# Fused attention, mixture of experts and FFN: hops and stores in steps of their own, one program order to the end, and weight splits spread over two steps

## The chip, the cores and the metric

The kernel runs on one core of a Trainium2 chip. The metric is the device time of one execution in microseconds. Before the change three runs took 1039.25, 1039.57 and 1040.21 us; their median is 1039.57 us.

## The reference

Three stages follow each other, all in float32, over 4 x 576 = 2304 tokens of 512 numbers:

```python
# linear attention, 8 heads of 64, with an RMS norm
kv = np.einsum('bhsd,bhse->bhde', k, v)
out = np.einsum('bhsd,bhde->bhse', q, kv)
out = out / np.sqrt(np.mean(out * out, axis=-1, keepdims=True) + 1e-06) * g_norm

# mixture of experts: the best 2 of 8 experts by noisy logits
for e in range(8):
    for k in range(2):
        mask = top2[:, k] == e
        h = np.maximum(x[mask] @ w1[e], 0.0)              # 512 -> 1024
        y[mask] += top2_w[mask, k, None] * (h @ w2[e])    # 1024 -> 512

# gated FFN, 512 -> 1536 -> 512
g = x @ w_gate
return (g / (1 + np.exp(-g)) * (x @ w_val)) @ w_out
```

Each expert has room for 640 tokens (`CAP`); tokens beyond that are handled by a branch, `spill`, that these inputs skip. The FFN's weights arrive as 64-bit floats.

## The kernel before, in words

**Precision.** Each float32 operand is split into a rounded half `hi` (written by ACT) and a remainder `lo` (a subtraction on DVE). A product is three matmuls on PE: hi·hi, hi·lo and lo·hi. `piece_split` (L624) does this for one piece of weights: L630 on ACT, then L632 on DVE, 128 x 1024 each.

**Blocks and steps.** The experts' tokens are worked in 16 blocks of 256 or 384 columns (`blocks`, L676 ff.): 256, 256, 384, 384, then 384, 256 four times, then 384, 384, 256, 256. A block has 8 steps. Step k computes `u` (`expert_up`, 12 matmuls, L752), from it `hh` on ACT (L761) and `hl` on DVE (L762), and runs `down` (L771) for step k-1: per 128 tokens three matmuls of 512 columns into `y`, with hh, hh and hl as the loaded operand. That makes 128 expert steps. Then the FFN runs in 6 groups `m` of 384 tokens with 12 steps each: `ug` and `uv` (12 matmuls each, L825), `sg`, `a` and `gl` on DVE, `gh` on ACT, and `down` again.

**What else a step does** stands in a table, `at(step, fn)` (L966 ff.):
- `piece_load` 3 or 4 steps ahead on SP (raw_w), and `piece_split` at the step itself.
- `narrow` (L650 ff.): 36 chunks that turn the FFN's weights from 64 to 32 bits. A DMA brings `d_..` in; three steps hold seven DVE operations (L658 to L668); the third also holds an addition on POOL (L669) and the DMA that stores the result (L670, SP). Chunks are spread over the 384-column blocks 2 to 13.
- `x_gather` (POOL, L701), then `x_quarters`: SP writes the gathered rows out as `xq` (L721) and reads them back turned by quarters (L722). This pair of DMAs is the hop.
- `x_halves` (L724): DVE transposes 32 x 32 blocks (`turn`, L691), ACT rounds (`xh`, L684), DVE subtracts (`xl`, L686): the operands of the next block.
- for the FFN the same with `y_mix` (two gathers), `y_sum` (ACT L801, DVE L802, then the hop) and `y_halves` (L691, L812, L813).
- `expert_out` stores y from ACT (L784, L787).
- `spill` (L861) after FFN step 1: four small DVE operations, a load of their result `toti` into a register of every engine (L869) and a branch on it (L870).

**Order.** `InOrder` (L31) keeps PE, ACT, DVE and SP in the program's order while `on` is set. It is set until step 16 (`PINNED`; the loop over `pinned` at L1152 clears it). From there to the end of the FFN the scheduler orders each engine's instructions by its own simulation. POOL is left to the scheduler throughout, since its `on` is never set. Buffers come from rings: tag "S" (6 of 128 x 1024, raw weights and `d_..`), tag "R" (5 of 128 x 512: xg, turn, f_.., ys, ya, yb).

Of the kernel before, what the change touches and what calls it, by code (L numbers as in the profile page):

```python
# [9 lines left out]
F32 = mybir.dt.float32  # L10
# [39 lines left out]
def attn_moe_ffn(ctx: ExitStack, tc: tile.TileContext, q, k, v, g_norm, w_gate, w_noise, noise, w1, w2,  # L50
# [32 lines left out]
        return wpool.tile([P, 1024], F32, name=nm, tag="W")  # L83

    def st_tile(nm):
        return pool.tile([P, 1024], F32, name=nm, tag="S", bufs=6)

    def row_tile(nm):
        return pool.tile([P, 512], F32, name=nm, tag="R", bufs=5)

    def xt_tile(nm):
        return pool.tile([P, 4, 384], F32, name=nm, tag="X", bufs=4)
# [555 lines left out]
    def narrow(src, dst, i):  # L648
        nm = f"{dst.name}_{i}"
        n = 512  # L650
        raw = st_tile("d_" + nm).bitcast(I32).rearrange("p (n t) -> p n t", t=2)
        SP.dma_start(raw.rearrange("p n t -> p (n t)"),
                          src.rearrange("a b -> (a b)").rearrange("(i p n) -> i p n", p=P, n=n)[i].bitcast(I32))
        f = row_tile("f_" + nm)
        fi, hw, lw = f.bitcast(I32), raw[:, :, 1], raw[:, :, 0]

        def one():
            V.tensor_scalar(fi, hw, 0x7FFFFFFF, None, op0=OP.bitwise_and)  # L658
            V.tensor_scalar(hw, hw, -2 ** 31, None, op0=OP.bitwise_and)
# [12 lines left out]
        return one, two, three


    blocks = [(0, 0, 256), (1, 0, 256), (0, 256, CAP - 256), (1, 256, CAP - 256)]
# [37 lines left out]
        gather_rows(x, xd[0:TP * P] if bk < 2 else xd, slot_tok[:, 0 if bk < 2 else 1, k:k + 1])  # L713
        XT[bk, "x", i] = x

    def x_quarters(bk, i):
        to_quarters(XT[bk, "x", i], f"xq{bk}_{i}")

    def to_quarters(x, nm):
        put, get = by_quarter(nm)  # L720
        SP.dma_start(put, x.rearrange("p (g k) -> p g k", g=4))  # L721
        SP.dma_start(x, get)  # L722

    def x_halves(bk, *tiles):  # L724
        if bk not in XT:
# [73 lines left out]
    def y_sum(t):  # L799
        a, b = XT.pop(("y", t))  # L800
        ACT.activation(a, a, AF.Copy, scale=wts[:, t, 0:1])  # L801
        V.scalar_tensor_tensor(b, b, wts[:, t, 1:2], a, op0=OP.mult, op1=OP.add)  # L802
        to_quarters(b, f"yq{t}")
        XT["y", t] = b

    def y_halves(t):
# [161 lines left out]
    def at(step, fn, *args):  # L968
        todo.setdefault(step, []).append((fn, args))

    starts = [NF * i for i in range(NB)]
    first_ffn = NF * NB
    for e in range(1, E):
        for i, (key, src, c) in enumerate(expert_pieces(e)):
            s0 = 7 + i if e == 1 else NF * 2 * (e - 1) + (i if e == E - 1 else 2 * i)
            at(s0 - 4, piece_load, key, src, c)
            at(s0, piece_split, key)
    for i, (key, src, c) in enumerate(ffn_pieces()):
        s0 = first_ffn - 14 + i if i < 15 else first_ffn - 10 + i
        at(s0 - 3, piece_load, key, src, c)  # L980
        at(s0, piece_split, key)
    if wide:
        halves = []
        for srcdst in ((u_gate, ug32), (u_val, uv32), (u_out, uo32)):
            halves += [(*srcdst, i) for i in range(DM * FU // (P * 512))]
        def start_narrow(i):
            XT["n", i] = narrow(*halves[i])

        slots = []
        for bk in range(2, NB - 1):  # L990
            slots += [starts[bk] + 8 * i // NARROW[blocks[bk][2]] for i in range(NARROW[blocks[bk][2]])]
        for i in range(len(halves)):
            st = slots[i * len(slots) // len(halves)]
            at(st - 4, start_narrow, i)
            for c in range(3):
                at(st + c, lambda i=i, c=c: XT["n", i][c]())
    for bk in range(2, NB):
        p = starts[bk - 1]
        n = blocks[bk][2] // P
        for i in range(n):  # L1000
            if bk > 2:
                at(p + 1, x_gather, bk, i)
            if bk > 3:
                at(p + 2 + i, x_quarters, bk, i)
            at(p + (5 if bk == 2 else 4) + i, x_halves, bk, i)
    for m in range(NM):
        p = first_ffn + NU * (m - 1) if m else first_ffn - NF - 3
        for i in range(3):
            lag = 2 * i + 2 if m else i + 1
            at(p + lag, y_mix, 3 * m + i)  # L1010
            at(p + lag + 2, y_sum, 3 * m + i)
            at(p + lag + 4, y_halves, 3 * m + i)

    def run_todo(step):
# [131 lines left out]
    for bk in range(NB):  # L1146
        for f in range(NF):
            st = starts[bk] + f
            if st == PINNED:
                later()  # L1150
                drain(routes)
                for x in pinned:  # L1152
                    x.on = False
            if st < PINNED:
                later()
                expert_up(bk, f)
# [59 lines left out]
```

## Time and profile before

| what | before |
|---|---|
| median of 3 runs | 1039.57 us |
| the profiled execution | 1039.84 us, its span 1038.2 us |
| busy in the span | PE 990.1 (95%), DVE 570.2 (55%), ACT 350.8 (34%), POOL 174.6 (17%) |
| PE's granted clock | 0.93 on average up to 145.93 us, 1.00 from there |
| expert blocks 2 to 15 | 145.93 to 573.15 us |
| FFN | 573.15 us to the end |

The profile comes from one execution and its span leaves out 1.64 us around it. "Busy" counts instructions that execute; an operation that waits in an engine's queue shows as idle time of that engine, with the name of what ended the wait (`<-`). DVEq, PEq and SPq are the engines' sequencers. Line numbers are those of the kernel before.

### The profile page before, as it was taken

The numbers are of one execution on the slowest core, as the hardware profiler recorded it, in microseconds if no ns is written. First come the engines' busy times: TensorE is split into PE (matmuls) and PEld (weight loads), VectorE is DVE, ScalarE is ACT, GpSimd is POOL, SyncE is SP. The second block draws the span as 40 slices with busy tenths as digits, with TensorE's granted clock in tenths as the row PEclk, the third lists the DMA queues.
The fourth block names the chain that finished last, engine by engine and source line by source line (L and its number), as shares of the span: only waits on it lengthen the run. The fifth ranks groups of instructions, "written<-read, shape, count | busy, mean of one in ns | idle before, by whom it ended". The sixth has DMA issues, their size and how long they took to land. (4 is left out here: it accounts for less than half of the span.)

```text
span 1038.2 us, 14809 instructions
## 1 busy us (share of the span) xinstructions
PE 990.1 (95%) x5689; PEld 894.6 (86%) x5690; DVE 570.2 (55%) x1080; ACT 350.8 (34%) x620; POOL 174.6 (17%) x171
## 2 busy tenths in 40 slices
PE   7988799998999999999999999999999999999998
PEld 7877687987898887889798979999999999999997
DVE  1869888687674758578637452342342432432222
ACT  3654434333524334352237331231321321321211
POOL 2414243322221221212221110100100100100000
PEclk9989899999999999999999999999999999999999
DMA  9995665866766767577657330310310310400000
GB/s 258 296 257 139 213 214 202 281 205 222 243 227 220 227 208 232 197 219 238 213 189 259 122 103 1 112 41 1 112 42 1 119 35 1 126 7 1 31 1 31
DMA packets 114508, 151.60 MB, mean 146 GB/s; under 512 B 15936, under 2 KB 75328, under 8 KB 114432
## 3 DMA queue, kind: packets, MB, share of 16 engines
q1 hardware_dynamic: 99536, 113.51, 35.8%
q0 software_dynamic: 6736, 22.29, 6.7%
q10 hardware_dynamic: 8160, 14.81, 4.0%
q8 instruction: 45, 0.74, 0.3%
q14 instruction: 31, 0.25, 0.1%
HBM read 108.64 MB, written 41.94 MB: 145 GB/s over the span
## 5 line engine op out<-in xcount | busy, mean ns | idle before, releaser
L752 PE MATMUL u<-xh,hi_w 128*128 128x384 f32 (+1 forms) x448 | 140.3, 314 | 2.2 <-ACT xh L684 2.2
L752 PE MATMUL u<-xl,hi_w 128*128 128x384 f32 (+1 forms) x448 | 140.4, 313 | 1.6 <-DVE xl L686 1.6
L752 PE MATMUL u<-xh,lo_w 128*128 128x384 f32 (+1 forms) x448 | 140.0, 313 | 0.0
L831 DVE TENSOR_TENSOR sg<-ug,sg 128x384 f32<-128x384 f32 x72 | 40.0, 555 | 154.2 <-ACT sg L830 154.2
L771 PE MATMUL y<-hi_w,hh 128*128 128x512 f32 x290 | 115.5, 398 | 5.0 <-ACT hh L761 4.8
L771 PE MATMUL y<-lo_w,hh 128*128 128x512 f32 x290 | 114.6, 395 | 0.0
L771 PE MATMUL y<-hi_w,hl 128*128 128x512 f32 x290 | 98.3, 401 | 5.4 <-DVE hl L762 5.2
L825 PE MATMUL uv<-mh,hi_uv 128*128 128x384 f32 x288 | 96.7, 336 | 1.6 <-DVE sg L831 1.4
L825 PE MATMUL ug<-mh,hi_ug 128*128 128x384 f32 x288 | 96.8, 336 | 0.4 <-PEq L870 0.4
L825 PE MATMUL ug<-mh,lo_ug 128*128 128x384 f32 x288 | 96.9, 336 | 0.0
L825 PE MATMUL uv<-mh,lo_uv 128*128 128x384 f32 x288 | 96.7, 336 | 0.0
L825 PE MATMUL ug<-ml,hi_ug 128*128 128x384 f32 x288 | 96.6, 335 | 0.0
L825 PE MATMUL uv<-ml,hi_uv 128*128 128x384 f32 x288 | 96.4, 335 | 0.0
L752 PEld LDWEIGHTS u<-xl,hi_w 128*128 128x128 f32 x448 | 84.4, 188 | 8.4 <-DVE xl L686 3.3
L752 PEld LDWEIGHTS u<-xh,hi_w 128*128 128x128 f32 x448 | 84.3, 188 | 8.0 <-ACT xh L684 3.9
L752 PEld LDWEIGHTS u<-xh,lo_w 128*128 128x128 f32 x448 | 84.4, 188 | 3.9
L834 ACT ACTIVATE gh<-a 128x384 fp32r<-128x384 f32 x72 | 37.8, 525 | 145.3 <-DVE a L832 145.3
L761 ACT ACTIVATE hh<-u 128x384 fp32r<-128x384 f32 (+1 forms) x113 | 49.0, 436 | 111.5 <-PE u L752 106.1
L830 ACT ACTIVATE sg<-ug 128x384 f32<-128x384 f32 x72 | 35.1, 488 | 151.7 <-PE ug L825 151.6
L632 DVE TENSOR_TENSOR lo_w<-raw_w,hi_w 128x1024 fp32r<-128x1024 f32 x48 | 61.9, 1290 | 37.1 <-ACT hi_w L630 37.1
L762 DVE SCALAR_TENSOR_TENSOR hl<-u,hh 128x384 fp32r<-128x384 f32 (+1 forms) x113 | 55.3, 489 | 36.7 <-ACT hh L761 36.7
L630 ACT ACTIVATE hi_w<-raw_w 128x1024 fp32r<-128x1024 f32 x48 | 50.9, 1059 | 68.1 <-DMA raw_w<-in_moe_w_dram 50.6
(420 smaller groups left out, 1993.5 us busy)
## 6 DMA issues: line engine op xcount, KB each, us to landing
raw_w<-in_moe_w_dram SPq DMA_DIRECT2D x56, 512.0 KB, 4.2
yd<-ys ACTq DMA_DIRECT2D x40, 256.0 KB, 2.7
xq<-xg SPq DMA_DIRECT2D x30, 256.0 KB, 3.8
xg<-xq SPq DMA_DIRECT2D x30, 256.0 KB, 4.4
d_ug<-in_moe_w_gate_dram SPq DMA_DIRECT2D x12, 512.0 KB, 4.6
d_uv<-in_moe_w_val_dram SPq DMA_DIRECT2D x12, 512.0 KB, 4.3
d_uo<-in_moe_w_out_dram SPq DMA_DIRECT2D x12, 512.0 KB, 4.4
yq<-yb SPq DMA_DIRECT2D x18, 256.0 KB, 2.7
```

The lines of the kernel that those rows point to most:

```text
L630: ACT.activation(hi.bitcast(F32R), raw, AF.Copy)
L632: V.tensor_sub(lo.bitcast(F32R), raw, hi)
L752: PE.matmul(pu, w[a][:, c, (f % 2) * P:(f % 2 + 1) * P], xs[b][:, c, 0:n], start=(k == 0), stop=(k == 11))
L761: ACT.activation(hi.bitcast(F32R), pu, AF.Relu)
L762: V.scalar_tensor_tensor(lo.bitcast(F32R), pu, 0.0, hi, op0=OP.max, op1=OP.subtract)
L771: PE.matmul(ACC[key][i], hs[a][:, i * P:(i + 1) * P], w[b][:, fi], start=(f == 0 and k == 0), stop=(f == nf - 1 and k == 2), skip_group_ch ...
L825: PE.matmul(pu, w[a][:, c, (f % 2) * P:(f % 2 + 1) * P], xs[b][:, c], start=(k == 0), stop=(k == 11))
L830: ACT.activation(sg, ps[0], AF.Sigmoid)
L831: V.tensor_mul(sg, ps[0], sg)
L834: ACT.activation(hi.bitcast(F32R), a, AF.Copy)
```

## The change

1. `x.on = False` at step 16 goes: PE, ACT, DVE and SP keep the program's order to the end.
2. The hop is split: `x_put` at step p-2+i and `x_get` at p+1+i (p is the first step of the block before; both were at p+2+i), and `x_gather` of blocks 4 and up moves from p+1 to p-4. `x_halves` stays at p+4+i. `y_get` gets a step of its own after `y_sum`.
3. The store of `narrow` gets a fourth step, one after the POOL addition.
4. `split_at` leaves `hi` at its step and puts `lo` one step later, for all pieces but those of expert 1.
5. Ring S has 7 buffers, ring R has 9, and `dynamic_dma_scratch_size` is set to 4096, which leaves room for them.

```diff
-        return pool.tile([P, 1024], F32, name=nm, tag="S", bufs=6)
+        return pool.tile([P, 1024], F32, name=nm, tag="S", bufs=7)
...
-        return pool.tile([P, 512], F32, name=nm, tag="R", bufs=5)
+        return pool.tile([P, 512], F32, name=nm, tag="R", bufs=9)
...
             POOL.tensor_add(f, f, lw.bitcast(F32))
+
+        def four():
             SP.dma_start(dst.rearrange("a b -> (a b)").rearrange("(i p n) -> i p n", p=P, n=n)[i], f)
...
         SP.dma_start(put, x.rearrange("p (g k) -> p g k", g=4))
-        SP.dma_start(x, get)
+        return lambda: SP.dma_start(x, get)
...
+    def split_at(step, key, apart=True):
+        if apart:
+            late = []
+            at(step, piece_split, key, late)
+            at(step + 1, lambda: V.tensor_sub(*late.pop()))
+        else:
+            at(step, piece_split, key)
...
-            at(s0, piece_split, key)
+            split_at(s0, key, e > 1)
...
-                at(p + 1, x_gather, bk, i)
+                at(p + 1 if bk < 4 else p - 4, x_gather, bk, i)
             if bk > 3:
-                at(p + 2 + i, x_quarters, bk, i)
+                at(p - 2 + i, x_put, bk, i)
+                at(p + 1 + i, x_get, bk, i)
...
+            at(p + lag + 3, y_get, 3 * m + i)
...
-                for x in pinned:
-                    x.on = False
...
-    nc = bacc.Bacc("TRN2", target_bir_lowering=False, num_devices=1)
+    nc = bacc.Bacc("TRN2", target_bir_lowering=False, num_devices=1, dynamic_dma_scratch_size=4096)
```

DVE, second half of block 11, where block 12's operands are made (`xl12`, from three x tiles) beside the `hl11` of the steps. Before:

```order
L691 STREAM_TRANSPOSE turn_4658<-xg12_0_4558 128x512
L762 SCALAR_TENSOR_TENSOR hl11_4_4644<-u11_4_4630,hh11_4_4643 128x256
L686 SCALAR_TENSOR_TENSOR xl12_4657<-turn_4658,gcol_73,xh12_4656 128x4x128
L632 TENSOR_TENSOR lo_w2_7_1_4916<-raw_w2_7_1_4756,hi_w2_7_1_4915 128x1024
L691 STREAM_TRANSPOSE turn_4693<-xg12_1_4560 128x512
L762 SCALAR_TENSOR_TENSOR hl11_5_4685<-u11_5_4671,hh11_5_4684 128x256
L632 TENSOR_TENSOR lo_w1_7_2_4957<-raw_w1_7_2_4785,hi_w1_7_2_4956 128x1024
L691 STREAM_TRANSPOSE turn_4729<-xg12_2_4562 128x512
L658 TENSOR_SCALAR f_uo32_117_3_4655<-d_uo32_117_3_4653 128x512
L686 SCALAR_TENSOR_TENSOR xl12_4657<-turn_4693,gcol_73,xh12_4656 128x4x128
L762 SCALAR_TENSOR_TENSOR hl11_6_4717<-u11_6_4703,hh11_6_4716 128x256
```

After:

```order
L44 SCALAR_TENSOR_TENSOR hl11_4_4647<-u11_4_4633,hh11_4_4646 128x256
L44 STREAM_TRANSPOSE turn_4660<-xg12_0_4386 128x512
L44 SCALAR_TENSOR_TENSOR xl12_4659<-turn_4660,gcol_73,xh12_4658 128x4x128
L44 SCALAR_TENSOR_TENSOR hl11_5_4690<-u11_5_4676,hh11_5_4689 128x256
L44 TENSOR_TENSOR lo_w1_6_3_4651<-raw_w1_6_3_4529,hi_w1_6_3_4650 128x1024
L44 STREAM_TRANSPOSE turn_4699<-xg12_1_4388 128x512
L44 SCALAR_TENSOR_TENSOR xl12_4659<-turn_4699,gcol_73,xh12_4658 128x4x128
L44 SCALAR_TENSOR_TENSOR hl11_6_4723<-u11_6_4709,hh11_6_4722 128x256
L44 STREAM_TRANSPOSE turn_4734<-xg12_2_4390 128x512
L44 SCALAR_TENSOR_TENSOR xl12_4659<-turn_4734,gcol_73,xh12_4658 128x4x128
L44 SCALAR_TENSOR_TENSOR hl11_7_4760<-u11_7_4746,hh11_7_4759 128x256
```

Before, `hl` and a weight remainder stand between a `turn` and its `xl`, and pieces of `narrow` (`f_uo32`) between two tiles. Now each `xl` follows its `turn` at once, and the next `hl` stands behind it.

SP, where the x tiles of a block make their hop among stores of `narrow` (`ug32`) and loads. Before, block 4:

```order
L721 DMA xq4_0_2295<-xg4_0_2247 128x4x128
L721 DMA xq4_1_2326<-xg4_1_2249 128x4x128
L722 DMA xg4_0_2247<-xq4_0_2295 128x512
L721 DMA xq4_2_2377<-xg4_2_2251 128x4x128
L722 DMA xg4_1_2249<-xq4_1_2326 128x512
L670 DMA ug32_115<-f_ug32_115_6_2123 128x512
L652 DMA d_ug32_115_11_2456<-in_moe2_w_gate_dram 128x1024
L622 DMA raw_w1_3_1_2523<-in_moe_w1_dram 128x4x256
L722 DMA xg4_2_2251<-xq4_2_2377 128x512
```

After, block 5:

```order
L44 DMA xq5_0_2465<-xg5_0_2378 128x4x128
L44 DMA ug32_115<-f_ug32_115_7_2214 128x512
L44 DMA xq5_1_2498<-xg5_1_2380 128x4x128
L44 DMA raw_w1_3_1_2529<-in_moe_w1_dram 128x4x256
L44 DMA ug32_115<-f_ug32_115_8_2258 128x512
L44 DMA d_uv32_116_0_2576<-in_moe2_w_val_dram 128x1024
L44 DMA xg5_0_2378<-xq5_0_2465 128x512
L44 DMA raw_w2_3_1_2612<-in_moe_w2_dram 128x2x512
L44 DMA d_uv32_116_1_2622<-in_moe2_w_val_dram 128x1024
L44 DMA xg5_1_2380<-xq5_1_2498 128x512
```

Before, one, two and four rows lie between the put (`xq4_i<-xg4_i`) and the get (`xg4_i<-xq4_i`) of tiles 0, 1 and 2. Now five and six lie between those of tiles 0 and 1.

DVE, the four operations of `spill`. Before, they stand in block 1, behind the count of the routed tokens (`base_f`):

```order
L44 TENSOR_TENSOR base_f_113<-base_f_113,rk2_1509 128x8
L44 TENSOR_TENSOR oh@2_1502<-oh@2_1502,rk@2_1545 128x144
L863 TENSOR_SCALAR over_6021<-base_f_113 128x8
L868 CAST cnti_6026<-base_f_113 128x8
L865 TENSOR_REDUCE tot_6023<-over_6021 128x1
L867 CAST toti_6025<-tot_6023 128x1
L44 SCALAR_TENSOR_TENSOR hl1_0_1550<-u1_0_1475,hh1_0_1549 128x256
```

After, they stand behind FFN step 1 (`a_1`, `gl_1`) and a weight remainder:

```order
L44 TENSOR_TENSOR sg0_1_5999<-ug0_1_5973,sg0_1_5999 128x384
L44 TENSOR_TENSOR a0_1_6000<-uv0_1_5986,sg0_1_5999 128x384
L44 TENSOR_TENSOR gl0_1_6005<-a0_1_6000,gh0_1_6004 128x384
L44 TENSOR_TENSOR lo_uo_4_5959<-raw_uo_4_5860,hi_uo_4_5958 128x1024
L44 TENSOR_SCALAR over_6021<-base_f_113 128x8
L44 TENSOR_REDUCE tot_6023<-over_6021 128x1
L44 CAST toti_6025<-tot_6023 128x1
L44 CAST cnti_6026<-base_f_113 128x8
L878 TENSOR_LOAD toti_6025
L879 COMPARE_AND_BRANCH
```

The result that all engines load before the branch is now made where the program has it, some 540 rows later on DVE.

## Rows read from the trace of the kernel before

**Rows 1.** The page's head: span of the profiled execution.

```profile
span 1038.2 us, 14809 instructions
```

**Rows 2.** Stretches of expert blocks 2 to 15: us, busy us of each engine, PE clock, DMA.

```profile
145.93:213.18 67.25, 64.93 (x332) 58.16 (x331) 54.17 (x100) 26.94 (x42) 19.59 (x12) 1.00 0.70 231
213.18:279.95 66.77, 61.04 (x323) 51.91 (x322) 49.09 (x75) 25.58 (x38) 15.73 (x12) 1.00 0.73 233
279.95:337.95 58.00, 57.56 (x315) 50.80 (x315) 38.67 (x66) 22.11 (x33) 11.85 (x9) 1.00 0.67 218
337.95:399.64 61.69, 57.43 (x311) 50.15 (x310) 41.25 (x67) 24.12 (x35) 13.19 (x11) 1.00 0.67 218
399.64:573.15 173.51, 169.94 (x932) 151.16 (x933) 121.17 (x197) 71.78 (x106) 38.25 (x31) 1.00 0.68 219
```

**Rows 3.** The chain of waits in a steady FFN step: start, us, what.

```profile
704.74 2.09 PE ug L825 x12
...
708.91 0.70 PE y('m', 1)_0_6938 L771 x3
```

**Rows 4.** Timeline of a 256-column step: start, us, engine, line.

```profile
560.84 0.39 ACT L761 ACTIVATE hh<-u 128x256 fp32r<-128x256 f32 x1
...
561.12 0.28 PE L752 MATMUL u<-xl,hi_w 128*128 128x256 f32 x1
...
561.24 0.28 PE L752 MATMUL u<-xh,lo_w 128*128 128x256 f32 x1
```

**Rows 5.** Line L825: durations, first and last start of one matmul of the FFN.

```profile
L825 PE MATMUL ug<-mh,hi_ug x288: 334/334/414, 573.1 to 1026.4; 128*128 128x384 f32 x144
```

**Rows 6.** Waits of ACT in two stretches, 213.18 to 279.95 and 337.95 to 399.64 us.

```profile
ACT hi_w L630 <- DMA raw_w<-in_moe_w_dram: 18.2, 6, 5.5
...
ACT hi_w L630 <- DMA raw_w<-in_moe_w_dram: 10.3, 4, 3.6
```

**Rows 7.** Waits of the whole span: us in total, times, longest us.

```profile
PE y L771 <- DVE hl L762: 5.2, 8, 1.4
...
DVE turn L691 <- DMA xg<-xq: 14.4, 11, 3.8
```

**Rows 8.** Waits of SP's queue: us in total, times, longest us.

```profile
SPq L670 <- POOL f_uo L669: 38.1, 9, 8.6
```

**Rows 9.** DMA issues: KB each, median us from issue to landing.

```profile
xg<-xq SPq DMA_DIRECT2D x30, 256.0 KB, 4.4
```

**Rows 10.** Timeline of one x tile: turn, then ACT's xh, then xl.

```profile
270.81 0.71 DVE L691 STREAM_TRANSPOSE turn<-xg 128x512 f32<-128x512 f32 x1 [1.79 <-issue]
...
271.55 1.23 ACT L684 ACTIVATE xh<-turn,gcol 128x512 fp32r<-128x512 f32 x1 [2.20 <-DVE turn L691]
...
272.81 1.16 DVE L686 SCALAR_TENSOR_TENSOR xl<-turn,gcol,xh 128x512 fp32r<-128x512 f32 x1 [0.99 <-ACT xh L684]
```

**Rows 11.** DVE's groups by shape: busy us, mean ns of one, idle before.

```profile
L632 DVE TENSOR_TENSOR lo_w<-raw_w,hi_w 128x1024 fp32r<-128x1024 f32 x48 | 61.9, 1290 | 37.1 <-ACT hi_w L630 37.1
...
L762 DVE SCALAR_TENSOR_TENSOR hl<-u,hh 128x384 fp32r<-128x384 f32 x64 | 35.0, 547 | 19.0 <-ACT hh L761 19.0
...
L762 DVE SCALAR_TENSOR_TENSOR hl<-u,hh 128x256 fp32r<-128x256 f32 x49 | 20.3, 413 | 17.7 <-ACT hh L761 17.7
...
L668 DVE SCALAR_TENSOR_TENSOR d_uo<-d_uo 128x512 f32<-128x512 uint32 x12 | 9.0, 746 | 0.1
```

**Rows 12.** Timeline around the branch and of the first spill operation.

```profile
118.77 0.17 DVE L863 TENSOR_SCALAR over<-base_f 128x8 f32<-128x8 f32 x1
...
584.51 0.56 DVE L832 TENSOR_TENSOR a<-uv,sg 128x384 f32<-128x384 f32 x1 [1.00 <-PE uv L825]
...
585.66 0.56 DVE L835 TENSOR_TENSOR gl<-a,gh 128x384 fp32r<-128x384 f32 x1 [0.59 <-ACT gh L834]
...
587.26 0.41 PE L825 MATMUL ug<-mh,hi_ug 128*128 128x384 f32 x1 [0.45 <-PEq L870]
```

**Rows 13.** Line L869: load of the register, by engine's queue.

```profile
L869 PEldq TENSOR_LOAD <-toti x1: 487/487/487, 585.7 to 585.7; - x1
```

More of the change, by code (lines that the diff above doesn't have):

```diff
@@ L669, in three @@
             POOL.tensor_add(f, f, lw.bitcast(F32))
+        def four():
             SP.dma_start(dst.rearrange("a b -> (a b)").rearrange("(i p n) -> i p n", p=P, n=n)[i], f)
-        return one, two, three
+        return one, two, three, four
     blocks = [(0, 0, 256), (1, 0, 256), (0, 256, CAP - 256), (1, 256, CAP - 256)]
@@ L714, in x_gather @@
         XT[bk, "x", i] = x
-    def x_quarters(bk, i):
-        to_quarters(XT[bk, "x", i], f"xq{bk}_{i}")
     def to_quarters(x, nm):
@@ L721, in to_quarters, with x_put, x_get @@
         SP.dma_start(put, x.rearrange("p (g k) -> p g k", g=4))
-        SP.dma_start(x, get)
+        return lambda: SP.dma_start(x, get)
+    def x_put(bk, i):
+        XT[bk, "q", i] = to_quarters(XT[bk, "x", i], f"xq{bk}_{i}")
+    def x_get(bk, i):
+        XT.pop((bk, "q", i))()
     def x_halves(bk, *tiles):
@@ L802, in y_sum, with y_get @@
         V.scalar_tensor_tensor(b, b, wts[:, t, 1:2], a, op0=OP.mult, op1=OP.add)
-        to_quarters(b, f"yq{t}")
+        XT["y", t] = b, to_quarters(b, f"yq{t}")
+    def y_get(t):
+        b, get = XT.pop(("y", t))
+        get()
         XT["y", t] = b
@@ L980, in attn_moe_ffn @@
         at(s0 - 3, piece_load, key, src, c)
-        at(s0, piece_split, key)
+        split_at(s0, key)
     if wide:
@@ L994, in attn_moe_ffn @@
             at(st - 4, start_narrow, i)
-            for c in range(3):
+            for c in range(4):
                 at(st + c, lambda i=i, c=c: XT["n", i][c]())
```

## Prediction

> **What bounds the kernel now.** I read the span first, then a table of stretches, then the chain and the waits of the stretches that are longer than their matmuls. The profiled span is 1038.2 us [rows 1]; that execution took 1.64 us more, 1039.84 us, and lies 0.27 us above the median of the runs. The reader is to see in the table that PE is busy nearly throughout [rows 2]. A busy PE isn't yet a PE at its pace, so I worked out the pace. In a steady step twelve matmuls of 384 columns take 2.09 us and the three matmuls of a 128-row y tile 0.70 us [rows 3]. An expert step of 384 columns is then 2.09 + 3 x 0.70 = 4.19 us, an FFN step 6.28 us. With 256 columns a matmul follows the last by 0.12 us [rows 4]; two thirds of 2.09 / 12 = 0.174 are 0.116, and I take that. There are two y tiles: 12 x 0.116 + 1.40 = 2.79 us.
>
> Blocks 2 to 15 would take 8 x (6 x 2.79 + 8 x 4.19) = 402.1 us; the five rows add up to 427.2 us, so 25.1 us are lost there. By stretch, eight steps to each block: 67.25 - 67.04 = 0.2; 66.77 - 55.84 = 10.9; 58.00 - 55.84 = 2.2; 61.69 - 55.84 = 5.9; 173.51 - 167.52 = 6.0 us [rows 2]. In the FFN the first matmul of its kind starts at 573.1 and the last at 1026.4 [rows 5]; the last one is the tenth of its step, so 1.57 us come off, and 451.7 us stand against 71 x 6.28 = 445.9: 5.8 us lost. Together **30.9 us** are there to be won. The front up to 145.93 us is in program order already.
>
> The two worst stretches, 16.8 of the 25.1 us, are also those in which ACT stands longest before a rounding whose raw weights haven't landed: 18.2 and 10.3 us [rows 6]. ACT's hh stands behind such a rounding, and PE's y behind hh or hl; PE names hl as the last thing it waits for in 5.2 us of it [rows 7]. The raw loads are late where SP is held: its queue waits up to 8.6 us before a store of narrow for the POOL addition just issued [rows 8], and loads and gets stand behind that store.
>
> **The change part by part.**
>
> *Store one step later; hop in two steps.* No instruction and no byte is added. The store now comes 2.8 or 4.2 us later. The raw loads, four steps ahead (11.2 us at least), keep 11.2 - 4.2 = 7 us of landing time even if SP is held for one step. The get stands three steps ahead of the turn: 3 x 2.79 = 8.4 us against a landing of 4.4 us [rows 9], 4.0 us in hand. I cost these waits at nothing from here on; the cover is that lead, and if it goes, the price is the last rival's. Ring S and R: the buffers taken were released two or three steps earlier in the printed order, so SP isn't held by them for more than a step, which the lead covers too; the bound is the same rival.
>
> *Splits in two steps.* ACT's rounding is done a step before DVE wants it, so DVE no longer waits for it. The wait doesn't stand on PE's path by itself; 0, bounds 0 to the 16.8 us that I count as removed below with the loads.
>
> *Program order.* This has a price. DVE now takes turn, xl and the next hl in that order, and xl waits for ACT's xh. One tile holds DVE from 270.81 to 273.97 us [rows 10], 3.1 us, with idle time in it that the scheduler had let an hl fill; pipelined with its neighbours I take 3.0. An hl is 0.41 or 0.55 us, a weight remainder 1.29 [rows 11]; each loses 0.07 us by overlap. PE's room: hl of step k is wanted by the third matmul of y(k), behind y(k-1), u(k+1) and two matmuls of 0.23: 2.10 + 2.09 + 0.47 = 4.66 us after u(k) has ended (3.27 us at 256 columns). hh (0.39 us at 256 columns, [rows 4]; some 0.1 more at 384), hl, their hand-overs and a weight load take about 1.55 and 1.25 us of it. So DVE may lag by **3.1 us** (384) or **2.0 us** (256) before PE stands.
>
> The lag then follows step by step (work minus step, what exceeds the room is PE's stall and shortens the lag). A 256 block before a 384 block, steps 4 to 7: work 3.4, 4.6 (with a remainder), 3.4, 1.6 against 2.8. Lag 0.6, 2.4, then a stall of 0.4, 2.6, a stall of 0.6: 0.9 us per block, four times. A 384 block before a 256 block also has narrow in it, 36 chunks in 48 steps with seven operations of up to 0.75 us [rows 11], some 2.2 us a step: work 5.8, 7.0, 2.6, 2.8 against 4.2 in steps 4 to 7. Lag 1.6, 4.4, stall 1.3: 1.3 us where narrow has chunks in both steps (blocks 6 and 10), 0 where not (4 and 8). The same sum gives 2.6 for block 3 (three tiles, 5.8, 7.0, 5.5), 3.6 for block 12 (three tiles and a remainder each step), 0.1 and 1.4 for 13 and 14, and 3.3 for block 15, whose mh and ml are made in a row. By the stretches above: 2.6, 0.9, 2.2, 0.9, 10.7, together **17.3 us**. Twelve PE transposes in block 2, in both kernels, add an estimated 12 x 0.12 = 1.4. With a room of 4 and 2.8 us, that is hand-overs at nothing, the same sum gives 8.9; with full means, no overlap and 3.1 us more exactly counted waits 29. I take 17.3 since the tile of [rows 10] is measured and the room worked out from steady rows.
>
> *The branch.* DVE made toti over 460 us before it was wanted; the operations cost 0.17 us and less each [rows 12]. Now they stand behind gl of FFN step 1 and one weight remainder. From the end of uv (a starts with it at 584.51) gl ends at 586.22 [rows 12], 1.8 us with its start lag of 0.1 counted; the remainder adds 1.2, three small operations 0.5: toti after 3.5 us. From PE's load of the register at 585.7 [rows 13] to its next matmul at 587.26 [rows 12] lie 1.56 us. PE is done with y after 2.09 us, and would start at 5.07: a stall of **3.0 us** in place of 0.45 [rows 12]. Bounds: 1.5 (if toti were there when y ends) and 4.5 (if ACT's gh comes late by a remainder's time). The load of the register is 0.487 us in this trace [rows 13], inside the 1.56. The Trainium skill (Runtime: NRT & Kernel Launch, "The ~15µs preamble/postamble breakdown") gives about 1.3 us for a TENSOR_LOAD as a round trip to HBM; by that the stall would be an estimated 0.8 us longer, 3.8. The trace's load is a third of that, and the sum goes by the trace. The rest of the FFN's 5.8 us I drop: in printed order each step is ug, uv, y, as in the steady ones [rows 3].
>
> *Front.* Two chunks of narrow that ran in block 1 now run later; 0, bound 1 us of gain.
>
> **Sum.** Lost after: 17.3 + 1.4 + 3.0 = 21.7 us; before 30.9. The span is 1038.2 - 9.2 = 1029.0, the run 1030.6, the median by the same 0.27 us **1030.4 us**.
>
> **The rivals.**
>
> *DVE's lag stays inside PE's room.* For it: the stretches that aren't worst held the same x tiles in the scheduler's order and lost 0.2 and 2.2 us [rows 2]. Against: there an hl passed between turn and xl. At 8.9 us in place of 17.3 the run would be 1022.0.
>
> *The lag eats the gain.* At 29 us in the blocks the loss is 29 + 1.4 + 3.0 = 33.4 us, 2.5 more than before: 1042. Against it: it needs every hand-over in full. Nearer its middle, 25 to 28, the time is that of before within the 0.2% (2.1 us) that a measurement of this kernel can tell from no change.
>
> *A held SP makes the get late, and in program order DVE stands with it: slower.* Before, DVE waited 14.4 us in 11 waits for gets [rows 7], beside which other work went on. In program order every hl behind such a turn waits too. It decides from 4.0 us of hold in front of a get in a 256 block (above); before, the store of narrow alone held SP up to 8.6 us [rows 8]. Then 14.4 us come on top where the lag already stands at the room: 1030.4 + 14.4 = **1044.8 us**. Against it: the store now follows its addition by a step, and no chunk of narrow begins in a 256 block.
>
> *It doesn't do what it says.* POOL stays with the scheduler, so gathers and additions may still come late; the printed order of PE, DVE, ACT and SP is the program's throughout. This would act through the late get and is counted there.
>
> **How the numbers follow.** The sum as worked out: 0.52. The lag inside the room: 0.20. The lag that eats the gain: 0.13, of which 0.09 within the 0.2% and 0.04 beyond it on the slow side. The late get: 0.15, of which 0.01 small enough to end as no change. Faster by over 0.2%: 0.72; within: 0.10; slower: 0.18. The range takes the deep room at its end and a little beyond (hand-overs at nothing and a branch at 1.5: 1020.5), and on the other side the lag at full means: 1019 to 1043. Outside are a later get and an all but hidden lag, some 2 in 10.
>
> **What would show it.** Right: ACT's wait for raw weights shrinks in both worst stretches; the second and fourth stretch come to 57 and 57 to 58 us; DVE stands before xl for xh in every tile; PE's waits for hl lie in steps 6 and 7 of a block and in the first of the next; one stall of about 3 us after the y of FFN step 0. Wrong: waits of DVE's turn for gets that don't shrink, SP held before a get for over 4 us, PE waits for hl over 25 us, or a stretch of blocks 10 to 15 that grows by more than 5 us.

## The result, and the profile after

The changed kernel takes **1053.7 us** (median of 4 runs, 1051.27 to 1056.33) against 1039.41 us before in the same runs: a ratio of 1.014, 95% interval 1.0112 to 1.0167. It is slower by 14 us, and outside the range of the prediction. The profiled execution took 1053.2 us, its span is 1051.5 us, 13.3 us more than before.

The stretches that answer to [rows 2], cut at the same block starts of the changed kernel's own trace (us, busy us of each engine, PE clock, DMA), and the FFN to the end of the span:

```profile
140.83:215.19 74.36, 69.19 (x346) 60.60 (x344) 59.31 (x109) 23.88 (x40) 16.27 (x13) 1.00 0.57 183
215.19:277.74 62.55, 60.93 (x316) 53.20 (x316) 46.72 (x72) 23.61 (x36) 14.09 (x11) 0.95 0.75 245
277.74:337.95 60.21, 57.51 (x312) 50.28 (x312) 40.69 (x63) 22.84 (x35) 11.48 (x9) 1.00 0.63 214
337.95:397.42 59.47, 57.58 (x312) 50.31 (x313) 45.50 (x70) 22.90 (x35) 12.38 (x10) 1.00 0.68 222
397.42:588.88 191.46, 176.82 (x937) 153.74 (x937) 135.35 (x204) 75.75 (x112) 36.58 (x29) 0.98 0.62 205
588.88:1051.50 462.62, 455.33 (x2383) 425.22 (x2381) 163.45 (x272) 113.97 (x198) 29.16 (x30) 1.00 0.16 50
```

The two stretches that I called the worst did get shorter, 66.77 to 62.55 and 61.69 to 59.47 us. The others grew: 67.25 to 74.36, 58.00 to 60.21 and 173.51 to 191.46 us. The first two stretches don't hold quite the same work in both kernels: before, y matmuls of block 3 still ran behind the first u of block 4, so the trace has 332 and 323 matmuls there, and now 346 and 316. At 0.23 us each I estimate that some 3 us of the first stretch's growth and some 2 us of the second's drop are that shift; it doesn't touch the sum. Blocks 2 to 15 take 448.05 us in place of 427.22, **20.8 us more**. PE's idle time in them grew by 9.7 us (16.3 to 26.0); the other 11.1 us are time in which PE counts as busy and gets on more slowly. Block 2 starts 5.1 us earlier (140.83), and the FFN's first matmul and the last of its kind, 588.9 and 1040.0 us, lie 2.2 us closer together than in [rows 5]. 20.8 - 5.1 - 2.2 is the 13.3 us within 0.2.

The waits of the whole span (us in total, times, longest us), to be held against [rows 7]:

```profile
ACT xh L44 <- DVE turn L44: 85.9, 30, 5.4
...
DVE xl L44 <- ACT xh L44: 50.1, 35, 3.2
...
PE u L44 <- ACT xh L44: 8.9, 6, 3.3
PE y L44 <- ACT hh L44: 8.7, 9, 2.2
PE y L44 <- DVE hl L44: 8.6, 16, 1.1
...
PE u L44 <- DVE xl L44: 3.9, 6, 0.7
```

Before, the rows of the same kind read (those of the part up to step 16, which was in program order already, have L44):

```profile
ACT xh L684 <- DVE turn L691: 59.7, 26, 8.7
...
DVE xl L686 <- ACT xh L684: 5.5, 7, 1.0
...
PE u L752 <- ACT xh L684: 2.2, 3, 1.2
...
PE u L752 <- DVE xl L686: 1.6, 3, 0.8
```

Two rows of before have no counterpart: ACT's wait for raw weights (18.2 and 10.3 us in two stretches, [rows 6]) and DVE's turn waiting for a get (14.4 us, [rows 7]). Neither is in the list of the changed kernel. What grew most on DVE is xl waiting for xh: 50.1 us against 5.5 and 7.4 more with L44. On PE it is u waiting for xh and xl, that is for the x tiles of the block that it is about to begin: 12.8 us against 3.8. PE's waits for hl, 8.6 us, are no more than before (5.2 in [rows 7] and 3.2 with L44); those for hh are 8.7 against 7.1. ACT stood long for turn before too, 59.7 us; there the scheduler chose what stood behind it.

How that comes about is seen at the end of block 11 (start us, us, engine, operation, idle before and what ended it; PE's rows shown only where it had stood):

```profile
452.25 0.70 DVE L44 STREAM_TRANSPOSE turn<-xg 128x512 f32<-128x512 f32 x1
...
452.99 1.23 ACT L44 ACTIVATE xh<-turn,gcol 128x512 fp32r<-128x512 f32 x1 [2.77 <-DVE turn L44]
...
454.12 0.37 ACT L44 ACTIVATE hh<-u 128x256 fp32r<-128x256 f32 x1
...
454.25 1.18 DVE L44 SCALAR_TENSOR_TENSOR xl<-turn,gcol,xh 128x512 fp32r<-128x512 f32 x1 [1.29 <-ACT xh L44]
...
455.35 0.41 DVE L44 SCALAR_TENSOR_TENSOR hl<-u,hh 128x256 fp32r<-128x256 f32 x1
...
455.68 0.70 DVE L44 STREAM_TRANSPOSE turn<-xg 128x512 f32<-128x512 f32 x1
...
456.41 1.19 ACT L44 ACTIVATE xh<-turn,gcol 128x512 fp32r<-128x512 f32 x1 [0.98 <-DVE turn L44]
...
457.63 1.09 DVE L44 SCALAR_TENSOR_TENSOR xl<-turn,gcol,xh 128x512 fp32r<-128x512 f32 x1 [1.25 <-ACT xh L44]
...
457.65 0.44 PE L44 MATMUL u<-xh,hi_w 128*128 128x384 f32 x1 [0.64 <-ACT xh L44]
...
458.78 0.45 PE L44 MATMUL u<-xl,hi_w 128*128 128x384 f32 x1 [0.69 <-DVE xl L44]
```

DVE turns a tile, stands 1.29 us until ACT has rounded it, subtracts, and only then gets to the hl that stands behind (455.35). ACT in its turn stood 2.77 us for the first of these turns, with hh of the next step queued behind it, and 0.98 us for the second. The last tile's xh is done at 457.60, and PE begins block 12 with it at once, after 0.64 us of standing, then stands 0.69 us more for xl. The tile itself is late, not only hl.

Behind the ends of blocks 3 and 12, with three tiles, narrow and remainders in the same steps, PE stands 3.02 and 3.31 us before the first u (at 215.19 and 497.29). There the clock goes with it (columns as above):

```profile
214.00:222.00 8.00, 6.36 (x18) 5.60 (x19) 4.86 (x8) 3.20 (x5) 1.29 (x1) 0.57 0.81 261
497.00:503.00 6.00, 4.99 (x18) 4.52 (x19) 5.67 (x7) 2.28 (x5) 1.42 (x1) 0.72 0.01 3
582.00:588.00 6.00, 5.12 (x21) 4.21 (x22) 4.01 (x5) 2.81 (x6) 0.00 (x0) 0.72 0.09 33
602.00:608.00 6.00, 4.41 (x16) 4.45 (x17) 0.21 (x2) 0.49 (x1) 0.94 (x1) 0.72 0.39 130
```

The granted clock is 0.57 on average over 8 us and 0.72 over three times 6 us: in part at the lower level, 1.2 in place of 2.4 GHz. Before, no stretch behind 145.93 us is under 1.00. The share not granted, 0.43 x 8 + 3 x 0.28 x 6, is 8.5 us; some of it falls on time in which PE stood anyway.

### The profile page after: what moved, and what is told of

Same layout as the page of the kernel before. It is cut to its first block, busy times and chain, and to the rows that moved or that the text cites. A ratio compares the mean times of both kernels' runs of the same rounds, so it can differ in the third digit from the quotient of the medians.

```text
span 1051.5 us, 14695 instructions
## 1 busy us (share of the span) xinstructions
PE 995.4 (95%) x5689; PEld 897.6 (85%) x5690; DVE 588.6 (56%) x1080; ACT 350.1 (33%) x620; POOL 166.0 (16%) x171
## 5 line engine op out<-in xcount | busy, mean ns | idle before, releaser
L44 PE MATMUL u<-xh,hi_w 128*128 128x256 f32 (+1 forms) x512 | 161.4, 315 | 9.0 <-ACT xh L44 8.9
L44 PE MATMUL u<-xl,hi_w 128*128 128x256 f32 (+1 forms) x512 | 160.8, 314 | 3.9 <-DVE xl L44 3.9
L44 PE MATMUL u<-xh,lo_w 128*128 128x256 f32 (+1 forms) x512 | 160.6, 314 | 0.3 <-DVE lo_w L44 0.3
L44 PE MATMUL y<-hi_w,hl 128*128 128x512 f32 x320 | 130.5, 408 | 8.7 <-DVE hl L44 8.6
L44 PE MATMUL y<-hi_w,hh 128*128 128x512 f32 x320 | 129.3, 404 | 8.7 <-ACT hh L44 8.7
L44 DVE TENSOR_TENSOR sg<-ug,sg 128x384 f32<-128x384 f32 x72 | 40.1, 557 | 169.9 <-ACT sg L44 169.8
L44 PE MATMUL y<-lo_w,hh 128*128 128x512 f32 x320 | 127.3, 398 | 0.0
L44 ACT ACTIVATE hh<-u 128x384 fp32r<-128x384 f32 (+1 forms) x128 | 55.4, 433 | 182.3 <-PE u L44 178.0
L44 PEld LDWEIGHTS u<-xh,hi_w 128*128 128x128 f32 x512 | 98.8, 193 | 17.5 <-ACT xh L44 11.5
L44 PEld LDWEIGHTS u<-xl,hi_w 128*128 128x128 f32 x512 | 98.8, 193 | 11.4 <-DVE xl L44 5.9
L44 DVE SCALAR_TENSOR_TENSOR hl<-u,hh 128x384 fp32r<-128x384 f32 (+1 forms) x128 | 61.9, 484 | 70.2 <-ACT hh L44 70.2
L44 PE MATMUL ug<-mh,hi_ug 128*128 128x384 f32 x288 | 97.4, 338 | 2.7 <-PEq L879 2.7
L44 PEld LDWEIGHTS u<-xh,lo_w 128*128 128x128 f32 x512 | 98.6, 193 | 0.5 <-DVE lo_w L44 0.5
L44 PE MATMUL ug<-mh,lo_ug 128*128 128x384 f32 x288 | 97.5, 338 | 0.0
L44 PE MATMUL ug<-ml,hi_ug 128*128 128x384 f32 x288 | 97.3, 338 | 0.0
L44 PE MATMUL uv<-mh,lo_uv 128*128 128x384 f32 x288 | 96.6, 336 | 0.0
L44 PE MATMUL uv<-mh,hi_uv 128*128 128x384 f32 x288 | 96.4, 335 | 0.0
L44 PE MATMUL uv<-ml,hi_uv 128*128 128x384 f32 x288 | 96.4, 335 | 0.0
L44 ACT ACTIVATE sg<-ug 128x384 f32<-128x384 f32 x72 | 35.3, 491 | 164.4 <-PE ug L44 160.7
L44 PEld LDWEIGHTS y<-hi_w,hl 128*128 128x128 f32 x320 | 60.6, 189 | 33.5 <-DVE hl L44 19.9
L44 ACT ACTIVATE gh<-a 128x384 fp32r<-128x384 f32 x72 | 37.8, 525 | 151.9 <-DVE a L44 151.9
L44 DVE TENSOR_TENSOR lo_w<-raw_w,hi_w 128x1024 fp32r<-128x1024 f32 x64 | 80.4, 1256 | 1.4 <-ACT hi_w L44 0.6
```

The costliest lines, as they stand in the source:

```text
L44: return self.tc.keep_in_program_order(fn(*args, **kw))
```

## The experiments

Ratios are to runs of the kernel before that were measured beside each run. Between the rows the median of the kernel before itself lay anywhere from 1038.78 to 1041.69 us, so medians of different rows can be off by 2 to 3 us against each other; the ratios take that out. Stretches come from the one profiled execution of each kernel.

| run | median us | ratio to before, 95% interval |
|---|---|---|
| the change | 1053.70 | 1.0140, 1.0112 to 1.0167 |
| e1: scheduler back from step 16 | 1019.57 | 0.9801, 0.9758 to 0.9844 |
| e3: x one step earlier | 1044.43 | 1.0036, 1.0012 to 1.0059 |
| e4: turn and xh a step before xl | 1050.31 | 1.0087, 1.0060 to 1.0113 |
| e5: branch's count early | 1053.30 | 1.0132, 1.0089 to 1.0176 |
| f1: before, rings 7 and 9 | 1016.74 | 0.9777, 0.9759 to 0.9796 |
| f2: e1, store in the third step | 1022.24 | 0.9828, 0.9805 to 0.9851 |
| f3: e1, hop together | 1017.93 | 0.9784, 0.9768 to 0.9801 |
| f4: e1, split in one step | 1021.85 | 0.9831, 0.9809 to 0.9853 |
| f5: before, ring R 9 | 1025.80 | 0.9851, 0.9818 to 0.9884 |
| f6: before, ring S 7 | 1038.31 | 0.9985, 0.9958 to 1.0012 |
| m1: before, x tiles in a ring of 4 | 1026.00 | 0.9851, 0.9826 to 0.9875 |
| k1: only DVE by scheduler | 1033.42 | 0.9932, 0.9909 to 0.9954 |
| k2: only ACT by scheduler | 1053.73 | 1.0123, 1.0081 to 1.0166 |
| k3: DVE and ACT by scheduler | 1043.06 | 1.0022, 1.0008 to 1.0037 |
| k4: DVE and PE by scheduler | 1028.38 | 0.9855, 0.9825 to 0.9884 |
| g1: x tile in three steps | 1025.07 | 0.9862, 0.9838 to 0.9886 |
| g2: g1, narrow apart | 1022.82 | 0.9850, 0.9825 to 0.9875 |
| h2: f1, program order in the FFN | 1013.58 | 0.9732, 0.9710 to 0.9754 |

**e1: the order alone undone.** The line that the change took out is put back.

```diff
                 drain(routes)
+                for x in pinned:
+                    x.on = False
```

> The changed kernel, but from step 16 on the scheduler orders PE, ACT, DVE and SP again; hop, store, split and rings stay as changed. Theory A (program order makes DVE stand in every x tile for ACT's xh, so the last tile of a block comes late for the next block's u): 1022 to 1041, no step of 9 us at the start of blocks 4 and 13. Theory B (the moved hop, the remainder a step later or the larger rings cost the time, whoever orders the work): 1050 or more. Theory C (program order costs little, the loss is SP standing in front of loads and gets): 1045 to 1055.

1019.57 us. Theory A stands (the time is 2 us below its range), B and C fall: program order alone costs some 34 us (1053.7 - 1019.6), and the rest of the change is worth 20 us. In e1's trace PE's u waits for no x tile any more. Its blocks 2 to 15 take 408.21 us in place of 448.05 and its FFN 465.99 in place of 462.62, so the price of program order lies in the blocks; in the FFN it gains a little. The changed kernel is two large effects of opposite sign.

**e3 and e4: the x tiles earlier.** In e3 all of x_halves of blocks 4 and up and the gets before them move one step; in e4 the gets, turn and xh move and xl stays.

```diff
-                at(p + 1 + i, x_get, bk, i)
-            at(p + (5 if bk == 2 else 4) + i, x_halves, bk, i)
+                at(p + i, x_get, bk, i)
+            at(p + (5 if bk == 2 else 4 if bk == 3 else 3) + i, x_halves, bk, i)
```

> The changed kernel with x_halves of blocks 4 to 15 and the gets before them one step earlier. Theory A: the losses at ten ordinary block ends (1.0 to 2.1 us each, some 16 together) go and the two ends of 8 us (blocks 3 and 12) shrink by a step of 4.2 each: 1029 to 1036. Theory B or C: 1051 to 1056, the stall only moves into another step.

> The changed kernel with turn and xh of blocks 4 to 15 one step earlier and xl where it was, so that DVE has a step's work between turn and xl instead of standing for xh (1.25 us in each of 27 tiles). Theory A: the block ends lose under 1 us each but those of blocks 3 and 12, which lose 2 to 5: 1024 to 1034, DVE's waits for xh under 10 us in place of 50. A rival of A, that only the due time counts and DVE's standing doesn't: as the run with x one step earlier, within 2 us. Theory B or C: 1051 to 1056.

```diff
+                at(p + 3 + i, lambda bk=bk, i=i, rest=rest: x_halves(bk, i, late=rest))
+                at(p + 4 + i, lambda rest=rest: lows(rest))
```

1044.43 and 1050.31 us: both gain, and both far less than theory A gave them. In e3 the x tiles come in time, and PE's u waits for none of them. But DVE and ACT stand for each other as before (ACT's xh for turn 91.3 us), and PE now stands longer for hl and hh, 24.0 us in place of 17.3:

```profile
DVE xl L44 <- ACT xh L44: 50.9, 35, 3.4
...
PE y L44 <- DVE hl L44: 12.5, 24, 1.1
...
PE y L44 <- ACT hh L44: 11.5, 14, 2.3
```

So the late tile is one part of the price, some 10 us of the 34; the standing is left as the cause of the rest, and g1 below puts that to the test. e4 takes DVE's standing for xh away (50 to 11 us), yet ACT stands as long for turn as ever, and now hl waits for hh. The waits of e4:

```profile
DVE hl L44 <- ACT hh L44: 104.8, 69, 7.1
ACT xh L44 <- DVE turn L44: 99.1, 30, 6.7
...
PE y L44 <- ACT hh L44: 20.4, 17, 2.6
...
DVE xl L44 <- ACT xh L44: 11.2, 5, 3.5
```

So one half of a mutual wait was taken away and the other kept: xh stands in ACT's queue in the same step as its turn, with the next hh behind it. That led to g1.

**g1 and g2: each tile over three steps, still in program order.**

```diff
+                at(p + 2 + i, lambda bk=bk, i=i, box=box: x_turn(bk, i, box))
+                at(p + 3 + i, lambda box=box: highs(box))
+                at(p + 4 + i, lambda box=box: lows(box))
...
-NARROW = {384: 6, 256: 0}
+NARROW = {384: (0, 1, 6, 7), 256: (0,)}
```

The last two lines, which place narrow by step of the block, are g2's alone, and the loop that reads them is changed to match. In both the get, put and gather of blocks 4 and up move earlier by two, one and one step.

> The changed kernel (program order to the end) with each x tile of blocks 4 to 15 spread over three steps: turn at p+2+i, xh at p+3+i, xl at p+4+i; get, put and gather earlier by two, one and one step. If program order costs what it does because DVE stands for xh and ACT, with hh behind it, for turn: 1020 to 1036, with ACT's waits for turn and DVE's for xh both under 30 us. If DVE's queue is late anyway through narrow and remainders ahead of hl: 1040 to 1050, and the waits move to hh and hl.

> As the run with x tiles in three steps, and the chunks of narrow begin at steps 0, 1, 6 and 7 of 384-column blocks and step 0 of 256-column blocks, away from most x steps. If narrow in front of turn and hl is the rest of what program order costs: 8 to 18 us less than that run. If it isn't: within 3 us of it.

1025.07 us, 28.6 us below the change, without giving one engine back to the scheduler. Both waits are small now (us in total, times, longest us), and blocks 4 to 9 run near their pace (stretches cut as in [rows 2], from block 4 on):

```profile
ACT xh L44 <- DVE turn L44: 14.1, 12, 2.6
...
DVE xl L44 <- ACT xh L44: 10.9, 5, 4.4
```

```profile
214.60:272.36 57.76, 57.17 (x316) 51.17 (x315) 48.27 (x74) 23.82 (x35) 14.52 (x11) 1.00 0.83 264
272.36:328.54 56.18, 56.18 (x314) 50.65 (x313) 40.60 (x63) 23.23 (x34) 10.31 (x9) 1.00 0.70 229
328.54:384.71 56.17, 56.17 (x313) 50.64 (x312) 45.08 (x70) 23.34 (x34) 12.95 (x10) 1.00 0.75 235
384.71:563.08 178.37, 171.96 (x937) 152.71 (x936) 133.00 (x202) 76.52 (x111) 36.86 (x29) 0.99 0.68 220
```

The pairs of blocks take 57.76, 56.18 and 56.17 us; 55.84 was the pace. Blocks 10 to 15 still lose 10.9 us (178.37 against 167.52; the changed kernel lost 23.9 there, the kernel before 6.0). g1 gives each hand-over a step and also starts turn two steps and xh one step earlier, while xl keeps its step. One step of lead alone was worth some 10 us (e3); no run gave two steps of lead with the tile in one step. g2 is 2.3 us lower with overlapping intervals: narrow in front of turn isn't the rest.

**k1 to k4: which engine's order.** One line of e1 each.

```diff
-                for x in pinned:
-                    x.on = False
+                V.on = False
```

(k2 `ACT.on`, k3 `V.on` and `ACT.on`, k4 `V.on` and `PE.on`.)

> The changed kernel with DVE alone given back to the scheduler from step 16; PE, ACT and SP stay in program order. If the 34 us between the changed kernel and the one with the scheduler back are DVE standing for xh and queueing narrow and remainders ahead of turn: 1020 to 1030. If ACT's order (hh behind xh) is the larger part: 1040 to 1050. If PE's strict order of u and y is: 1048 to 1056.

> The changed kernel with ACT alone given back to the scheduler from step 16; PE, DVE and SP stay in program order. If DVE's order is the cost: 1042 to 1054. If it is ACT's hh behind xh: 1022 to 1034. If the two stand for each other, so that freeing either helps: 1030 to 1042 here and with DVE freed.

> The changed kernel with DVE and ACT given back to the scheduler from step 16; PE and SP in program order. DVE alone gave 20 of the 34 us that program order costs. If the other 14 are ACT and DVE standing for each other: 1019 to 1025. If they are PE's own order (y strictly behind the next u, so that a late hl stops PE): 1030 to 1036.

> The changed kernel with DVE and PE given back to the scheduler; ACT and SP in program order. If PE's own order is the rest: 1019 to 1025. If it is ACT's: 1029 to 1036.

DVE freed alone gives 20 of the 34 us (1033.42), ACT alone nothing (1053.73). PE freed beside DVE gives 5 more (1028.38). The times of k1 and k4 fall between the cases that were set up for them. Freeing ACT beside DVE is *worse* than DVE alone (1043.06), which none of the cases expected. In the profiled executions the blocks of k3 take no longer than those of k1 (432.29 and 434.15 us), but its FFN does, 463.65 against 458.85 us: 4.8 of the 9.6 us between the medians are seen there. The rest is open, as k1's profiled execution is 3.6 us above its median and k3's 2.5 below. So these runs show that DVE's order is the largest part, not a sum of parts by engine.

**f1, f5, f6, m1: what was worth 20 us.** On the kernel before, only the rings are changed (f1 both lines, f5 the second, f6 the first) and, as in the change, the scratch of 4096 is set; m1 keeps R at 5 and S at 6 and gives the gathered x tiles four buffers of their own. f6 has the scratch too and gains nothing, so the scratch isn't what the others gain by.

```diff
-        return pool.tile([P, 1024], F32, name=nm, tag="S", bufs=6)
+        return pool.tile([P, 1024], F32, name=nm, tag="S", bufs=7)
...
-        return pool.tile([P, 512], F32, name=nm, tag="R", bufs=5)
+        return pool.tile([P, 512], F32, name=nm, tag="R", bufs=9)
```

```diff
-        x = row_tile(f"xg{bk}_{i}")
+        x = pool.tile([P, 512], F32, name=f"xg{bk}_{i}", tag="G", bufs=4)
```

> The kernel before with rings of 7 and 9 buffers and the scratch of 4096, nothing else. Theory A (what was gained under the scheduler came from SP no longer standing before stores and puts, so that raw weights land earlier): 1035 to 1042. Theory D (the rings alone let loads and gathers start earlier): 1018 to 1030.

> The kernel before with ring R at 9 buffers and the scratch of 4096, ring S at 6. If R (x tiles, turned tiles, chunks of narrow, y tiles) was what held the loads and gets: 1015 to 1022. If it was S (raw weights): 1034 to 1041.

> The kernel before with ring S at 7 buffers and the scratch of 4096, ring R at 5. If R was it: 1034 to 1041. If S was it: 1015 to 1022. If both are needed, this run and the one with R alone both lie between, 1023 to 1033.

> The kernel before with the gathered x tiles in a ring of their own of 4, ring R at 5, ring S at 6, scratch 4096: as many buffers as with R at 9 (1025.8 us). If R was short because x tiles wait in it from gather to turn behind chunks of narrow and y tiles: 1018 to 1028. If other users of R were short: 1034 to 1041.

f1 takes 1016.74 us: theory A fell and theory D holds. The rings alone give as much as the whole change does under the scheduler. R at 9 gives 1.5%, S at 7 nothing that can be told from no change, both together 2.2%. As many buffers with the x tiles apart give the same as R at 9 (1026.00 and 1025.80): it is enough to take the x tiles out of the five buffers that they shared with the other users. The trace of before shows this sharing. Its gathers of x wait for stores of narrow, though they read nothing of them; what the tiles have in common in the program is ring R:

```profile
POOL xg L701 <- DMA uv<-f_uv: 7.4, 3, 3.1
...
POOL xg L701 <- DMA ug<-f_ug: 5.9, 2, 3.8
...
POOL xg L701 <- DMA uo<-f_uo: 4.6, 3, 1.9
```

f6, with R still at 5, has the same three rows (5.9, 7.6 and 5.1 us); f1, f5 and m1 have none of them. The stretches of f1 answer to [rows 2]:

```profile
144.61:208.94 64.33, 64.33 (x331) 58.42 (x330) 58.01 (x108) 28.11 (x43) 17.91 (x11) 1.00 0.77 259
208.94:267.54 58.60, 58.60 (x324) 52.65 (x323) 41.11 (x69) 25.58 (x37) 14.67 (x12) 1.00 0.78 255
267.54:324.06 56.52, 56.52 (x313) 50.23 (x311) 37.43 (x62) 22.68 (x35) 9.33 (x7) 1.00 0.66 211
324.06:381.73 57.67, 56.75 (x314) 50.67 (x313) 40.64 (x71) 23.21 (x35) 15.57 (x12) 1.00 0.76 245
381.73:550.76 169.03, 169.03 (x936) 152.00 (x937) 118.90 (x199) 72.25 (x108) 38.10 (x29) 1.00 0.66 217
```

They add up to 406.15 us, against 427.22 before and a pace of 402.1; PE is busy through four of the five. Two causes aren't told apart by these runs. The larger ring lets gathers, turns and chunks of narrow start earlier on the chip; and the scheduler, which knows the rings, writes another order. ACT's wait for raw weights isn't the measure of it: m1 and before have the same, and m1 is 1.5% faster; in f6 the row is down to 23.5 us in 12 waits, and f6 is no faster. First before, then m1:

```profile
ACT hi_w L630 <- DMA raw_w<-in_moe_w_dram: 50.6, 23, 5.5
```

```profile
ACT hi_w L630 <- DMA raw_w<-in_moe_w_dram: 51.0, 26, 6.8
```

**f2, f3, f4: the other parts, each undone in e1.**

```diff
-                at(st + c, lambda i=i, c=c: XT["n", i][c]())
+                at(st + min(c, 2), lambda i=i, c=c: XT["n", i][c]())
...
-                at(p - 2 + i, x_put, bk, i)
-                at(p + 1 + i, x_get, bk, i)
+                at(p + 2 + i, x_put, bk, i)
+                at(p + 2 + i, x_get, bk, i)
...
-            split_at(s0, key, e > 1)
+            split_at(s0, key, False)
```

(f2 the first piece; f3 the second, with gather and y_get put back as well; f4 the third, for the FFN's pieces as well.)

> The kernel with the scheduler back (1019.6 us), the store of narrow again in the step of its POOL addition. Theory A: SP stands before the stores again; 1026 to 1036. If the store's place doesn't matter to the scheduler's order: 1018 to 1022.

> The kernel with the scheduler back (1019.6 us), gather, put and get where they were before the change. Theory A: DVE's turns wait for gets again (14 us before) and loads stand behind puts; 1024 to 1032. If the hop's place doesn't matter: 1018 to 1022.

> The kernel with the scheduler back (1019.6 us), hi and lo of every weight piece in one step again. By the forecast's step (DVE's wait for the rounding doesn't stand on PE's path by itself): 1018 to 1023. If spreading the split was what let the rest run: 1026 or more.

1022.24, 1017.93 and 1021.85 us beside 1019.57 of e1, all with overlapping intervals of the ratio. By the medians none of the three moves is worth more than 3 us under the scheduler, and the hop's may cost 1.6; e1's interval alone is 9 us wide (0.9758 to 0.9844), so a few us more can't be excluded for one of them. Together they gain nothing that can be seen: e1 has all three and the rings, f1 the rings alone, and f1's median is the lower one. What they are worth in program order alone wasn't tried one by one.

**e5 and h2: the branch.** e5 is the changed kernel with the four operations at step 18. h2 is f1 with program order from the FFN's first step on, and the same early count.

```diff
+    at(PINNED + 2, spill_count)
...
+    for x in pinned:
+        x.on = True
     for m in range(NM):
```

> The changed kernel with the four small DVE operations in front of the branch moved to step 18, 460 us before the branch; the branch stays. If the branch costs what the trace names (PE stands 2.7 us for it and the next FFN step takes 9.1 us): 2 to 4 us less than the changed kernel, 1050 to 1052. If PE would stand there anyway for DVE: no change, 1053 to 1055.

> The kernel before with rings of 7 and 9, the scheduler from step 16 to the end of the blocks, program order in the FFN, and the branch's four DVE operations at step 18. The first seven FFN steps lose 4.7 us under the scheduler and 0.3 in the run with the early count in program order: 1011 to 1015. If the blocks' end pays for it: 1016 to 1019.

e5's median doesn't move (1053.3). Its FFN does: from the first ug to the end of the span 458.85 us in place of 462.62, while its block 2 starts at 144.5 in place of 140.83 us with the same instructions ahead of it. Among the kernels here block 2 starts anywhere from 140.8 to 146.0 us, one execution each, which can hide 3.8 us; whether e5's later start is chance or comes with its edit, one trace doesn't show. In h2 the FFN takes 458.87 us, 4.8 less than f1's 463.64, and the median is **1013.58 us**, the fastest of all and 2.7% below before (0.971 to 0.9754). The FFN's rows, e5, f1, h2:

```profile
592.85:1051.70 458.85, 453.76 (x2383) 423.65 (x2381) 163.00 (x268) 113.99 (x198) 29.14 (x30) 1.00 0.16 50
```

```profile
550.76:1014.40 463.64, 456.05 (x2385) 423.72 (x2383) 161.01 (x268) 111.88 (x197) 32.33 (x30) 1.00 0.16 49
```

```profile
548.83:1007.70 458.87, 453.80 (x2383) 423.69 (x2381) 162.16 (x268) 113.98 (x197) 29.42 (x30) 1.00 0.16 50
```

## Why the prediction was wrong, point by point

- **Pace and loss before.** Right: 25.1 us above the pace in the blocks. f1's blocks take only some 4 us more than that pace. The split by stretch was less exact: part of block 3's y ran in the second stretch, so the first lost more than 0.2 us and the second less than 10.9.
- **"The raw loads are late where SP is held ... by the store", and the gain put down to store and hop.** This step failed. By the medians store and hop are worth less than 3 us each (f2, f3). The late raw weights in [rows 6] were real and disappeared, but they weren't the price: m1 keeps them and is faster, f6 has half of them and isn't. Nor does SP stand less before the stores: in the changed kernel it waits for the POOL additions 36 times, 175.6 us together and up to 13.7, before 23 times, 92.6 us and up to 8.7. The loads land in time all the same.
- **Rings at nothing.** This is where the gain was: 2.2% by f1, most of it R. I bounded the rings by what SP would wait for a buffer and never asked what the shortage of before had cost. The trace of before names no ring as such, but its gathers waited for stores of narrow that share one with them (17.9 us in 8 waits), and I didn't ask why.
- **"PE's room: hl of step k".** This step failed most. I let DVE's lag cost only through hl and forgot two things that stand in the same order. The x tile has a due time of its own: the next block's first u wants xh and xl. And ACT is in order too: xh stands for turn with hh behind it, 85.9 us in 30 waits, while DVE stands for xh. Neither half pays alone (ACT freed alone gains nothing in k2, e4 3 to 6 us); giving every hand-over its own step gained 29 (g1). The terms came to 17.3 + 1.4 = 18.7 us; measured are 448.05 - 402.1 = 46 us, with at most 6.8 us of them clock (0.43 x 8 + 2 x 0.28 x 6), a term that the forecast didn't have. By stretch I had 4.0, 0.9, 2.2, 0.9 and 10.7 us; it lost 7.3, 6.7, 4.4, 3.6 and 23.9. Of my signs of being wrong one came clearly, blocks 10 to 15 grew by 18.0 us; PE's waits for hl stayed at 8.6 us, far under the 25 that I had named, and PE stood 12.8 us for xh and xl, which no sign covered.
- **The branch.** Right: 3.0 us of stall forecast, 2.70 measured, and the FFN loses 449.5 - 445.9 = 3.6 us. The load of the register on PE's queue takes 0.488 us. The 1.3 us that the Trainium skill (Runtime: NRT & Kernel Launch, "The ~15µs preamble/postamble breakdown") gives are for loads from HBM at the launch, not for this load from a tile of the kernel; the 0.8 us more that I worked out from them did not come.
- **The front.** Forecast 0 to -1, measured -5.1; e5 with the same front has -1.4. The seven kernels here with DVE in program order start block 2 at 140.8 to 145.3 us (median 141.6), the thirteen others at 142.2 to 146.0 (median 144.5): some 3 us may come with the order, the rest is scatter.
- **The rivals.** The slower one, a late get, didn't occur: no turn waits for one. "The lag eats the gain" had the sign of it and 29 us for the blocks; they lost 46.

What stays open: how much of the rings' gain is buffers and how much the scheduler's other order, how much of g1's gain is the earlier turn, and half of what makes k3 slower than k1.

## What to carry to other kernels

Where two engines hand a tile to and fro and both keep a fixed order, give every hand-over a step of its own: half of it (e4) gained 3 to 6 us, all of it (g1) 29. When a lag is followed by hand, list every reader of the late engine's results with its due time, those of the next block included. And when a change has several parts, put a price on the dull one too: here larger rings were worth as much as the whole change under the scheduler, though in the trace of before they showed only as gathers that waited for the stores of other tiles.

## What was not expected of the hardware

PE's granted clock, at 1.00 for the whole time behind the front before, fell after four stalls of the changed kernel: after PE had stood 3.02 us at 215.19, 3.31 at 497.29, 1.95 and 0.45 at 582.43 and 583.61, and 2.70 us at the branch. A stall of about 3 us thus cost up to 0.43 x 8 = 3.4 us again in matmuls at the lower level, as these rows of PE show behind the first of them (the last two are matmuls of 512 columns, the first of them slow, the other fast):

```profile
215.19 0.69 PE L44 MATMUL u<-xh,hi_w 128*128 128x384 f32 x1 [3.02 <-ACT xh L44]
...
220.02 0.63 PE L44 MATMUL y<-hi_w,hh 128*128 128x512 f32 x1
...
222.34 0.39 PE L44 MATMUL y<-lo_w,hh 128*128 128x512 f32 x1
```

Without the stall at the branch e5's FFN is 3.8 us shorter, 1.1 more than the stall itself; that fits a slower stretch behind it, but no run took the clock's part away by itself.
